# A linear-attention and feed-forward kernel: the first batch's keys loaded without a cast, its queries ahead of its values, and its first tile's pieces in another order

## The chip, the cores and the metric

The kernel runs on one core of one Trainium2 chip. The metric is the device time of one execution in microseconds (us); lower is better. The engines are named as in the profile: PE is TensorE's matmuls and PEld its weight loads, DVE is VectorE, ACT is ScalarE, POOL is GpSimd, SP is SyncE. SPq and POOLq mark the issue of a DMA by SP or POOL.

## The reference, cut to what matters

Eight batches of eight heads, 576 positions and 64 channels go through a cosine-weighted linear attention. The result, 4608 tokens by 512, goes through a feed-forward with a product of two branches.

```python
def phi(x, c, s):                      # c, s: cos and sin of pi/2 * pos / 576
    r = np.maximum(x, 0.0)
    return np.concatenate([r * c, r * s], axis=-1)
q_p, k_p = phi(q, cos_w, sin_w), phi(k, cos_w, sin_w)
kv  = np.einsum('bhsf,bhsd->bhfd', k_p, v)
num = np.einsum('bhsf,bhfd->bhsd', q_p, kv)
den = np.einsum('bhsf,bhf->bhs', q_p, k_p.sum(axis=2))[..., None] + 1e-06
x   = (num / den).transpose(0, 2, 1, 3).reshape(4608, 512)
out = (((x @ w1) * (x @ w2)) @ w3) @ w_out
```

Inputs and output are float32; the kernel computes in bf16 with float32 accumulation.

## The kernel before, in words

**Attention of a batch.** The 576 positions of a batch are five chunks, four of 128 rows and one of 64 (`c = 0..4`). A chunk's keys become features `kp`: DVE writes the cosine half with one max-and-multiply, ACT writes the sine half with a scaled Relu. Values go into `va` beside a column of ones, so that one product of `kp` with `va` gives `kv` and the denominators' sums together. The result is copied to `kvs` in bf16. A chunk's queries become features `qp` in the same way, are transposed by PE through PSUM (`pst`) into `qpT`, and multiplied with `kvs`. DVE divides by the denominators into `xblk`. PE transposes `xblk`, and a copy brings it into `xT`, the layout in which the feed-forward reads it.

**Feed-forward.** The tokens are nine tiles of 512. `ffn_groups(t)` is a generator that issues tile `t`'s matmuls: products with `w1b` and `w2b` (L512), their elementwise product `abT` (L517, L518, or L557, L561), then the product with `w34b` (L583), which is `w3 @ w_out` formed once in the kernel (L239, L251). After each group it yields, and the attention work that is planned for this slot (`at(s, ...)`) is issued behind it. So the program order of every engine is written by hand, and each engine runs its own instructions strictly in that order.

**The head of the kernel**, which the change touches, is a straight list at the end of the function, for batch 0 alone. The loads of batch 0 come in pieces. SP loads the first four heads' keys, chunks 0 to 3, as float32 without a cast (`kf` number 0, the first half), and the keys of chunk 4 (`k4`). POOL loads everything else and casts to bf16 on the way, in this order: values of the first four heads, values of chunk 4, queries of chunks 0 and 1, keys of the last four heads (`kf` number 1, the second half), values of the last four heads, queries of chunks 2 and 3, then the weights. While nothing has arrived, PE runs products of zeros (`idle_mms`, L198).

In the list, `first_keys(half)` makes four heads' key features, `first_values(half)` copies their values, `first_kv(half)` forms their `kv`; `first_num(c, half)` is four heads' numerator of a chunk, and the function that it returns normalizes it on DVE; `q_tr_halves` and `q_tr` transpose a chunk of queries (with `evac=False`, the entry `[1]` of what `q_tr` returns is the copy by ACT); `num(0, 2)` and `num(0, 3)` are whole chunks; `x_tr` brings a chunk into `xT`. `other_loads` issues the remaining weights behind the second half's `kvs`.

**Tile 0** is treated apart (`first_tile`): its 512 tokens are the chunks 0 to 3 of batch 0, and the first two column pairs are computed chunk by chunk (`chunk`), each as soon as its `xT` is there. Before the change the slots in it run so: half of chunk 0, `num(0, 2)`, the rest of chunk 0, `x_tr` of chunk 1 with `q_tr` of chunk 3, chunk 1 with its `multiply`, `x_tr` of chunk 2 and `num(0, 3)`, chunk 2, half of `on_half(0, 1)`, `x_tr` of chunk 3, the rest of it, chunk 3. `multiply` is an ACT copy out of PSUM (L517) and a DVE product (L518).

Of the kernel before, what the change touches and what calls it, by code (L numbers as in the profile page):

```python
# [16 lines left out]
P = 128  # L17
H, S, D = 8, 576, 64
F = 2 * D
# [49 lines left out]
def kernel(  # L69
# [85 lines left out]
    def load_half(eng, t, src, half, heads):  # L155

        rows = src[0, ts(half, 4), 0:512, :].rearrange("h (p j) d -> p h (j d)", j=4)
        eng.dma_start(out=t[:, heads, 0:4, :].rearrange("p h j d -> p h (j d)"), in_=rows)  # L158


    k0 = [wst.tile([P, 4, 4, D], dt, name=f"kf{i}") for i, dt in enumerate((FP32, BF16))]
    k4 = wst.tile([P, H, D], FP32, name="k4")
    q0 = raw[0, "q"] = ld.tile([P, H, NCH, D], BF16, name="qs", bufs=2)
    v0 = raw[0, "v"] = ld.tile([P, H, NCH, D], BF16, name="vs")
    load_half(nc.sync, k0[0], k, 0, slice(0, 4))
    nc.sync.dma_start(out=k4[0:64, :, :], in_=k[0, :, 512:S, :].rearrange("h p d -> p h d"))
    zeros = const.tile([P, 512], BF16, name="zeros")
    nc.vector.memset(zeros[:], 0.0)
    cosv, sinv = _trig_tables(nc, const)
    load_half(nc.gpsimd, v0, v, 0, slice(0, 4))  # L170
    va_bufs, kp_bufs, qp_bufs = [], [], []

# [22 lines left out]
    def idle_mms(n):  # L195

        for _ in range(n):
            nc.tensor.matmul(unread[:, :], lhsT=zeros[:, 0:128], rhs=zeros[:], start=True, stop=True)  # L198

    idle_mms(17)  # L200
    load_first4(nc.gpsimd, v0, v)
    load_first(nc.gpsimd, q0, q, 0, 2)
    load_half(nc.gpsimd, k0[1], k, 1, slice(0, 4))
    identb = const.tile([P, P], BF16, name="identb")
    make_identity(nc, identb[:])
    load_half(nc.gpsimd, v0, v, 1, slice(4, 8))
# [96 lines left out]
    def prep_q(b, c):  # L303
        features(b, feat_of(b)[1], raw[b, "q"], c)
        if c in dma_q(b):
            transpose_q(b, c)
# [18 lines left out]
            nc.vector.tensor_copy(out=kvs[:, 4:8, :], in_=kvt[:, 1, 0:260])  # L325
            att[b]["kvs"] = kvs

    def first_keys(half):
        kp = feat_of(0)[0]
        for c in range(4):  # L330
            src, heads = k0[half][:, :, c, :], ts(half, 4)
            nc.vector.tensor_scalar(out=kp[:, c, heads, 0:D], in0=src, scalar1=0.0,
                                    scalar2=cosv[:, c:c + 1], op0=ALU.max, op1=ALU.mult)
            nc.scalar.activation(out=kp[:, c, heads, D:F], in_=src, func=ACTF.Relu,
                                 scale=sinv[:, c:c + 1], bias=0.0)
        if half == 0:
            nc.vector.tensor_scalar(out=kp[0:64, 4, :, 0:D], in0=k4[0:64], scalar1=0.0,
                                    scalar2=cosv[0:64, 4:5], op0=ALU.max, op1=ALU.mult)
            nc.scalar.activation(out=kp[0:64, 4, :, D:F], in_=k4[0:64], func=ACTF.Relu,
                                 scale=sinv[0:64, 4:5], bias=0.0)  # L340

    def first_values(half):
        heads = ts(half, 4)
# [162 lines left out]
    def ffn_groups(t):  # L506
        x = xT[t]
        abT = fsb.tile([P, 8, 512], BF16, name="abT", bufs=2)

        def products(out, w, jc, tok):  # L510
            for kc in range(4):
                nc.tensor.matmul(out, lhsT=w[:, kc, ts(jc, 128)], rhs=x[:, kc, tok],  # L512
                                 start=(kc == 0), stop=(kc == 3))

        def multiply(a, b, pair, half):
            asb = fsb.tile([P, 512], BF16, name="asb")
            nc.scalar.copy(out=asb[:], in_=a[:, :])  # L517
            nc.vector.tensor_mul(out=abT[:, ts(pair, 2), ts(half, 256)],  # L518
                                 in0=asb[:].rearrange("p (i n) -> p i n", i=2),
                                 in1=b[:, :].rearrange("p (i n) -> p i n", i=2))  # L520

        def chunk(a, b, c):

            for i in range(2):
                for ps, w in ((a, w1b), (b, w2b)):
                    products(ps[:, ds(256 * i + 128 * (c % 2), 128)], w, i, ts(c, 128))
                if c == 0 and i == 0:
                    yield

        def on_half(half, pair):  # L530
            a, b = ffn_tile(), ffn_tile()
            for ps, w in ((a, w1b), (b, w2b)):
                for i in range(2):
                    products(ps[:, ts(i, 256)], w, 2 * pair + i, ts(half, 256))
                if w is w1b and not (t == 0 and half == 1):
                    yield
            multiply(a, b, pair, half)
            yield

        def first_tile():  # L540

            banks = [(ffn_tile(), ffn_tile()) for _ in range(2)]
            for c in range(4):
                if c == 3:
                    yield from on_half(0, 1)
                yield from chunk(*banks[c // 2], c)
                if c % 2:
                    multiply(*banks[c // 2], 0, c // 2)
                yield
            yield from whole(4)  # L550
            yield from on_half(1, 1)

        def whole(jc):
            aT = ffn_tile()
            products(aT[:, :], w1b, jc, slice(0, 512))
            asb = fsb.tile([P, 512], BF16, name="asb")
            nc.scalar.copy(out=asb[:], in_=aT[:, :])  # L557
            yield
            bT = ffn_tile()
            products(bT[:, :], w2b, jc, slice(0, 512))  # L560
            nc.vector.tensor_mul(out=abT[:, jc, :], in0=asb[:], in1=bT[:, :])  # L561
            yield

        if t == 0:
            yield from first_tile()
        elif t == 1:
            for half in range(2):
                for pair in range(2):
                    yield from on_half(half, pair)
        for jc in range((5, 4)[t] if t < 2 else 0, 8):  # L570
            yield from whole(jc)
        if t == 0:
            for jp in range(8):
                for part in range(2):
                    w34_mm(jp, part)
                    yield
            early.close()
            holds.append(ctx.enter_context(tc.tile_pool(name="hold", bufs=HELD,
                                                        reuse_waits="tile")))
        for ms in range(3 if t == NT - 1 else 4):  # L580
# [12 lines left out]
            yield  # L593
        if t == NT - 1:
            for half in range(2):
                cols = ts(half, 256)
                ops = ffn_tile()
                for jc in range(8):
                    nc.tensor.matmul(ops[:, 0:256], lhsT=abT[:, jc, ts(3, 128)],  # L599
                                     rhs=w34b[:, jc, cols], start=(jc == 0), stop=(jc == 7))  # L600
                nc.scalar.copy(out=osb[:, 1, cols], in_=ops[:, 0:256])
                store(nc.sync, osb[:, 1:2, :], 4 * t + 3, 1, cols)
                yield
# [6 lines left out]
    def at(s, *calls):  # L610
        slots[s] += calls
# [26 lines left out]
            at(s, issue)  # L638


    first_keys(0)
    first_values(0)
    first_kv(0)
    q0f = feat[0][1]
    prep_q(0, 0)
    prep_q(0, 1)
    idle_mms(2)
    q_tr_halves(0, 0)
    first_keys(1)
    halves = [first_num(0, 0)]  # L650
    q_tr(0, 1, evac=False)[1]()
    first_values(1)
    halves[0]()
    features(0, q0f, q0, 2, sin=False)
    first_kv(1)
    halves.append(first_num(1, 0))
    halves.append(first_num(0, 1))
    halves[1]()
    halves[2]()
    features(0, q0f, q0, 2, cos=False)  # L660
    q_tr(0, 2, evac=False)[1]()
    other_loads(att[0]["kvs"][:, 4, 0:1])
    halves.append(first_num(1, 1))
    x_tr(0, 0, by_vector=True)
    halves[3]()
    first.close()
    ps_ffn.append(ctx.enter_context(tc.tile_pool(name="ps_ffn1", bufs=2, space=bass.MemoryType.PSUM)))
    features(0, q0f, q0, 3)


    at(0, lambda: num(0, 2))
    at(1, lambda: x_tr(0, 1), lambda: q_tr(0, 3, evac=False)[1]())
    at(2, lambda: x_tr(0, 2, by_vector=True), lambda: num(0, 3))
    at(4, lambda: x_tr(0, 3))
    at(6, lambda: nc.vector.memset(qp_bufs[0][64:128, 4, :, :], 0.0))
    at(19, lambda: features(0, q0f, q0, 4))
# [73 lines left out]
```

## Time and profile before

| | us |
|---|---|
| median of 14 runs | 250.88 (250.54 to 252.68) |
| the profiled execution | 250.72 |
| its span in the profile | 249.0 |
| PE busy, with 1843 matmuls | 238.8 (96%) |
| DVE / ACT / POOL busy | 137.2 / 132.7 / 95.6 |
| first matmul of tile 0 | 16.37 |
| start of tile 0's fifth column block, `whole(4)` | 25.51 |
| last matmul's end | 245.84 |

The profiled execution took 250.72 us, 1.7 us more than its span; that part lies before and after what the profile records. Times within the span count from its start. A row of a timeline has start, duration, engine, line, operation, output and inputs, how many instructions were merged, and in brackets how long the engine had been idle and what released it. TensorE's granted clock is full speed in all forty slices of the span.

### The profile page before, as it was taken

To read this page: it belongs to the slowest core of one execution; us is meant where nothing else is said; L and a number is where in the kernel's file an instruction comes from. 1 tells how busy PE (TensorE), PEld (TensorE's weight loads), DVE (VectorE), ACT (ScalarE), POOL (GpSimd) and SP (SyncE) were. 2 spreads that over 40 slices of the span, in tenths; PEclk is the share of its full clock that TensorE was granted. 3 is DMA by queue.
4 is the path that set the end of the run, shared out by engine and by line. 5 is a ranking of instruction groups with operands and counts; after the bars stand their busy time and mean duration, and the time that the engine had idled before them with its cause. 6 is when DMAs were issued, how large, how long until landed. Compare 5 with 4: busy or idle time off the path is not lost.

```text
span 249.0 us, 5001 instructions
## 1 busy us (share of the span) xinstructions
PE 238.8 (96%) x1843; PEld 129.4 (52%) x1843; DVE 137.2 (55%) x347; ACT 132.7 (53%) x273; POOL 95.6 (38%) x198
## 2 busy tenths in 40 slices
PE   8578999999999999999999999999999999999994
PEld 3367545566875445454554554455545554444443
DVE  6684473486978634737575566447466635312420
ACT  7663323784954684367546644855575433434332
POOL 8773352034521341225142612173204005978700
PEclk9999999999999999999999999999999999999999
DMA  6999999999999979699999799989995436898923
GB/s 131 180 196 200 207 204 204 194 141 155 197 143 151 154 125 180 87 131 156 113 182 165 109 184 149 156 135 155 152 145 95 95 65 209 248 294 286 290 88 130
DMA packets 86232, 40.96 MB, mean 165 GB/s; under 512 B 53824, under 2 KB 82752, under 8 KB 86208
## 3 DMA queue, kind: packets, MB, share of 16 engines
q0 software_dynamic: 37552, 27.47, 71.6%
q1 hardware_dynamic: 48656, 13.18, 34.8%
q8 instruction: 14, 0.23, 0.4%
q14 instruction: 10, 0.08, 0.1%
HBM read 38.80 MB, written 9.44 MB: 194 GB/s over the span
## 4 chain that ended last, share of the span: by engine, by line
PE 91%; DMA 3%; POOL 2%; DVE 1%; ACT 1%; issue 0%; POOLq 0%
PE ffnps L512 50%; PE ffnps L583 24%; PE ffnps L251 6%; PE pnum L415 4%; PE pnum L319 4%; DMA qs<-in_q_dram 3%; PE pst L239 1%; PE ffnps L599 1%; PE pst L467 1%; POOL vs L158 1%; PE pst L389 1%; ACT asb L517 0%; ACT qpT L392 0%; POOL qs L133 0%; DVE xblk L379 0%
## 5 line engine op out<-in xcount | busy, mean ns | idle before, releaser
L512 PE MATMUL ffnps<-xT,w1b 128*128 128x512 bf16 (+2 forms) x336 | 75.0, 348 | 2.1 <-DVE xT L469 1.5
L512 PE MATMUL ffnps<-xT,w2b 128*128 128x512 bf16 (+2 forms) x336 | 75.0, 348 | 0.0
L561 DVE TENSOR_TENSOR abT<-asb,ffnps 128x512 bf16<-128x512 bf16 x64 | 43.9, 686 | 52.8 <-PE ffnps L512 52.3
L583 PE MATMUL ffnps<-w34b,abT 128*128 128x512 bf16 x280 | 65.0, 379 | 0.0
L557 ACT CAST asb<-ffnps 128x512 bf16<-128x512 f32 x64 | 37.4, 584 | 50.7 <-PE ffnps L512 45.8
L512 PEld LDWEIGHTS <-w1b 128*128 128x128 bf16 x336 | 30.6, 98 | 28.6 <-issue 2.6
L512 PEld LDWEIGHTS <-w2b 128*128 128x128 bf16 x336 | 30.7, 98 | 27.4
L618 POOL COPY seen<-mark 1x1 bf16<-1x1 bf16 x50 | 8.9, 177 | 82.9 <-ACT mark L616 82.8
L583 PEld LDWEIGHTS <-abT 128*128 128x128 bf16 x280 | 26.0, 98 | 27.9 <-DVE abT L561 0.2
L590 ACT COPY osb<-ffnps 128x512 f32<-128x512 f32 x35 | 20.5, 584 | 35.8 <-PE ffnps L583 35.8
L288 ACT ACTIVATE qp<-qs,sinv 128x512 bf16<-128x512 bf16 (+1 forms) x40 | 28.3, 720 | 0.0
L311 POOL COPY va<-vs 128x512 bf16<-128x512 bf16 (+1 forms) x30 | 17.8, 626 | 26.0 <-DMA vs<-in_v_dram 17.9
L433 DVE TENSOR_TENSOR xblk<-pnum,den 128x512 bf16<-128x512 f32 (+1 forms) x36 | 24.9, 691 | 1.2
L288 ACT ACTIVATE kp<-ks,sinv 128x512 bf16<-128x512 bf16 (+1 forms) x35 | 25.0, 717 | 0.3 <-DMA ks<-in_k_dram 0.3
L497 POOL DMA_DIRECT2D out_dram<-osb x42 | 22.1, 531 | 2.2 <-issue 2.1
L415 PEld LDWEIGHTS <-qpT 128*128 128x128 bf16 x304 | 14.8, 98 | 8.1
L431 DVE TENSOR_SCALAR den<-pnum 128x8 f32<-128x8 f32 (+1 forms) x36 | 5.9, 163 | 22.3 <-PE pnum L415 22.0
L284 DVE TENSOR_SCALAR qp<-qs,cosv 128x512 bf16<-128x512 bf16 (+1 forms) x40 | 17.0, 435 | 0.7 <-DMA qs<-in_q_dram 0.6
L251 PE MATMUL ffnps<-woutb,w3T 128*128 128x512 bf16 x64 | 15.9, 380 | 0.0
L415 PE MATMUL pnum<-kvs,qpT 128*128 128x65 bf16 x288 | 15.4, 194 | 0.0
L319 PEld LDWEIGHTS <-kp 128*128 128x128 bf16 x280 | 11.4, 98 | 4.1
L284 DVE TENSOR_SCALAR kp<-ks,cosv 128x512 bf16<-128x512 bf16 (+1 forms) x35 | 12.8, 374 | 0.0
(96 smaller groups left out, 183.9 us busy)
## 6 DMA issues: line engine op xcount, KB each, us to landing
out_dram<-osb POOLq DMA_DIRECT2D x16, 256.0 KB, 4.2
out_dram<-osb POOLq DMA_DIRECT2D x24, 128.0 KB, 3.7
vs<-in_v_dram POOLq DMA_DIRECT2D x8, 256.0 KB, 5.9
qs<-in_q_dram POOLq DMA_DIRECT2D x8, 256.0 KB, 6.3
ks<-in_k_dram POOLq DMA_DIRECT2D x6, 320.0 KB, 5.5
qs<-in_q_dram POOLq DMA_DIRECT2D x6, 320.0 KB, 5.9
vs<-in_v_dram POOLq DMA_DIRECT2D x6, 320.0 KB, 5.9
ks<-in_k_dram POOLq DMA_DIRECT2D x6, 256.0 KB, 6.4
```

The lines of the kernel that those rows point to most:

```text
L251: nc.tensor.matmul(acc[:, :], lhsT=w3T[:, lc, :], rhs=woutb[:, lc, :], start=(lc == 0), stop=(lc == 7))
L284: nc.vector.tensor_scalar(out=dst[:R, c, :, 0:D], in0=src[:R, :, c, :], scalar1=0.0, scalar2=cosv[:R, at:at + 1], op0=ALU.max, op1=ALU.mult)
L288: nc.scalar.activation(out=dst[:R, c, 0:n, D:F], in_=src[:R, 0:n, c, :], func=ACTF.Relu, scale=sinv[:R, at:at + 1], bias=0.0)
L319: nc.tensor.matmul(kvt[:, h // 4, ds((h % 4) * 65, 65)], lhsT=kp[:, c, h, :], rhs=va[:, c, h, 0:D + 1], start=(i == 0 and h % 4 == 0), sto ...
L415: nc.tensor.matmul(banks[h // 4][:, ds((h % 4) * 65, 65)], lhsT=qpT[:, h, ds(at, 128)], rhs=kvs[:, h, :], start=True, stop=True)
L433: nc.vector.tensor_tensor(out=xblk[rows, g], in0=n4[:, :, :, 0:D], in1=den[rows, g].unsqueeze(3).to_broadcast([R, G, 4, D]), op=ALU.mult)
L497: eng.dma_start(out=rows[:, :, cols], in_=osb[64 * i:64 * i + rows.shape[0], :, cols])
L512: nc.tensor.matmul(out, lhsT=w[:, kc, ts(jc, 128)], rhs=x[:, kc, tok], start=(kc == 0), stop=(kc == 3))
L557: nc.scalar.copy(out=asb[:], in_=aT[:, :])
L561: nc.vector.tensor_mul(out=abT[:, jc, :], in0=asb[:], in1=bT[:, :])
L583: nc.tensor.matmul(ops[:, :], lhsT=abT[:, jc, ts(ms, 128)], rhs=w34b[:, jc, :], start=(jc == 0), stop=(jc == 7))
L590: nc.scalar.copy(out=osb[:, ms % 2, :], in_=ops[:, :])
```

## The change

Four things are altered, all in the head and in tile 0.

- **Loads.** Both halves of batch 0's keys are loaded in float32 by SP, the second between the first and `k4`. On POOL's queue the second half of the keys is gone, and the queries of chunks 0 and 1 come first, ahead of the values.
- **The list.** All key features come first, those of the second half included. The second half's sine features are shared out: chunks 0, 1 and 2 by ACT, chunk 3 by DVE. The features of query chunks 0 and 1 come between them, then the transposes, and only then values and `kv`. The features of query chunk 2 go ahead of the first normalization on DVE, those of chunk 3 ahead of the last one.
- **Idle products.** Twenty-five at the start instead of seventeen, and the two in the list are gone.
- **Tile 0.** `num(0, 2)` runs ahead of the first chunk. Chunk 1 is given a yield in its middle and chunk 2 loses the one at its end, so `x_tr` of chunk 2 comes in the middle of chunk 1, ahead of chunk 1's `multiply`, and `num(0, 3)` behind chunk 1.

```diff
-    k0 = [wst.tile([P, 4, 4, D], dt, name=f"kf{i}") for i, dt in enumerate((FP32, BF16))]
+    k0 = [wst.tile([P, 4, 4, D], FP32, name=f"kf{i}") for i in range(2)]
...
-    load_half(nc.sync, k0[0], k, 0, slice(0, 4))
+    for half in range(2):
+        load_half(nc.sync, k0[half], k, half, slice(0, 4))
     nc.sync.dma_start(out=k4[0:64, :, :], in_=k[0, :, 512:S, :].rearrange("h p d -> p h d"))
...
+    load_first(nc.gpsimd, q0, q, 0, 2)
     load_half(nc.gpsimd, v0, v, 0, slice(0, 4))
...
-    idle_mms(17)
+    idle_mms(25)
     load_first4(nc.gpsimd, v0, v)
-    load_first(nc.gpsimd, q0, q, 0, 2)
-    load_half(nc.gpsimd, k0[1], k, 1, slice(0, 4))
...
-    def first_keys(half):
+    def first_keys(half, cos=(), sin=(), sin_by_vector=()):
...
+        for c in sin_by_vector:
+            R, heads, src = of(c)
+            nc.vector.tensor_scalar(out=kp[R, c, heads, D:F], in0=src, scalar1=0.0,
+                                    scalar2=sinv[R, c:c + 1], op0=ALU.max, op1=ALU.mult)
...
-                if c == 0 and i == 0:
+                if c < 2 and i == 0:
                     yield
...
-                yield
+                if c != 2:
+                    yield
...
-    first_keys(0)
+    q0f = feat_of(0)[1]
+    first_keys(0, cos=range(4), sin=range(4))
+    first_keys(1, cos=range(5), sin=(4, 0))
+    features(0, q0f, q0, 0)
+    first_keys(1, sin_by_vector=(3,))
+    features(0, q0f, q0, 1)
+    first_keys(1, sin=(1, 2))
+    q_tr_halves(0, 0)
+    by_scalar = q_tr(0, 1, evac=False)[1]
     first_values(0)
     first_kv(0)
-    q0f = feat[0][1]
-    prep_q(0, 0)
-    prep_q(0, 1)
-    idle_mms(2)
-    q_tr_halves(0, 0)
-    first_keys(1)
+    by_scalar()
     halves = [first_num(0, 0)]
-    q_tr(0, 1, evac=False)[1]()
     first_values(1)
+    features(0, q0f, q0, 2, sin=False)
     halves[0]()
-    features(0, q0f, q0, 2, sin=False)
     first_kv(1)
     halves.append(first_num(1, 0))
+    halves[1]()
     halves.append(first_num(0, 1))
-    halves[1]()
     halves[2]()
     features(0, q0f, q0, 2, cos=False)
-    q_tr(0, 2, evac=False)[1]()
+    by_scalar = q_tr(0, 2, evac=False)[1]
     other_loads(att[0]["kvs"][:, 4, 0:1])
     halves.append(first_num(1, 1))
     x_tr(0, 0, by_vector=True)
+    by_scalar()
+    features(0, q0f, q0, 3)
     halves[3]()
     first.close()
...
-    features(0, q0f, q0, 3)
-
-
-    at(0, lambda: num(0, 2))
+    num(0, 2)
+
+
     at(1, lambda: x_tr(0, 1), lambda: q_tr(0, 3, evac=False)[1]())
-    at(2, lambda: x_tr(0, 2, by_vector=True), lambda: num(0, 3))
+    at(2, lambda: x_tr(0, 2, by_vector=True))
+    at(3, lambda: num(0, 3))
     at(4, lambda: x_tr(0, 3))
```

More of the change, by code (lines that the diff above doesn't have):

```diff
@@ L326, in kv_chunk, with of @@
             att[b]["kvs"] = kvs
-    def first_keys(half):
+    def first_keys(half, cos=(), sin=(), sin_by_vector=()):
         kp = feat_of(0)[0]
[L330 to L340, printed above, removed]
+        def of(c):
+            if c < 4:
+                return slice(0, P), ts(half, 4), k0[half][:, :, c, :]
+            return slice(0, 64), slice(0, H), k4[0:64]
+        for c in cos:
+            R, heads, src = of(c)
+            nc.vector.tensor_scalar(out=kp[R, c, heads, 0:D], in0=src, scalar1=0.0,
+                                    scalar2=cosv[R, c:c + 1], op0=ALU.max, op1=ALU.mult)
+        for c in sin:
+            R, heads, src = of(c)
+            nc.scalar.activation(out=kp[R, c, heads, D:F], in_=src, func=ACTF.Relu,
+                                 scale=sinv[R, c:c + 1], bias=0.0)
+        for c in sin_by_vector:
+            R, heads, src = of(c)
+            nc.vector.tensor_scalar(out=kp[R, c, heads, D:F], in0=src, scalar1=0.0,
+                                    scalar2=sinv[R, c:c + 1], op0=ALU.max, op1=ALU.mult)
     def first_values(half):
```

## The prediction

> **What bounds the kernel now.** First the stretches: the busy time of each engine up to tile 0's first matmul, from there to the start of `whole(4)`, and from there to PE's end.
>
> ```profile
> 0.00:16.37 16.37, 10.95 (x103) 6.02 (x104) 11.66 (x51) 11.92 (x22) 12.45 (x26) 1.00 1.20 165
> 16.37:25.51 9.14, 7.52 (x116) 6.93 (x116) 4.91 (x14) 4.13 (x7) 4.88 (x8) 1.00 1.40 199
> 25.51:245.84 220.33, 220.29 (x1624) 116.47 (x1623) 120.68 (x284) 116.31 (x245) 78.30 (x166) 1.00 1.06 164
> ```
>
> The first figure after the stretch is its length, the second PE's busy time. From 25.51 us on PE is idle for 0.04 us in 220. The change leaves those matmuls alone. So the time follows the start of `whole(4)` one to one, as long as no later load comes too late; everything is decided in the first 25 us. There I read the chain that ended last, then the timeline.
>
> ```profile
> 6.16 7.50 DMA qs<-in_q_dram
> 16.37 0.61 PE ffnps L512 x8
> 20.07 0.69 DVE abT L518
> 24.87 0.59 ACT asb L517
> ```
>
> ```profile
> 7.36 0.72 ACT L339 ACTIVATE kp<-k,sinv 64x512 bf16<-64x512 f32 x1 [0.99 <-DMA k<-in_k_dram]
> 9.55 0.94 DVE L284 TENSOR_SCALAR qp<-qs,cosv 128x512 bf16<-128x512 bf16 x2 [0.63 <-DMA qs<-in_q_dram]
> 10.38 0.61 PE L402 MATMUL pst<-identb,qp 128*128 128x128 bf16 x8 [0.68 <-ACT qp L288]
> 13.68 0.35 DVE L284 TENSOR_SCALAR qp<-qs,cosv 128x512 bf16<-128x512 bf16 x1
> 15.12 1.01 ACT L392 COPY qpT<-pst 128x1024 bf16<-128x1024 bf16 x1 [0.71 <-PE pst L389]
> 20.67 0.42 DVE L469 COPY xT<-pst 128x512 bf16<-128x512 bf16 x1
> 21.14 0.38 PE L512 MATMUL ffnps<-xT,w1b 128*128 128x128 bf16 x4 [1.02 <-DVE xT L469]
> ```
>
> The chain runs through the load of query chunks 2 and 3, landing at 13.66, and then through short steps to 16.37. In tile 0 PE loses 1.02 us, because the copy of chunk 2 into `xT` (20.67) stands on DVE behind chunk 1's `multiply` (20.07).
>
> The DMA view, by issue and by queue, gives the landings. First the two loads by SP with size and time to landing; then packets, MB and share of each queue in the stretches 3.75 to 4.25, 7.75 to 8.25 and 5.75 to 6.75.
>
> ```profile
> kf<-in_k_dram SPq DMA_DIRECT2D x1, 512.0 KB, 3.8
> k<-in_k_dram SPq DMA_DIRECT2D x1, 128.0 KB, 6.1
> ```
>
> ```profile
> q1 hardware_dynamic: 209, 0.07, 55.6%
> ```
>
> ```profile
> q0 software_dynamic: 362, 0.09, 185.7%
> ```
>
> ```profile
> q0 software_dynamic: 340, 0.12, 103.7%
> q1 hardware_dynamic: 91, 0.02, 17.5%
> ```
>
> SP's queue (q1) moves 209 packets in 0.5 us while it is alone, and 91 in 1.0 us beside POOL's casting queue (q0). Issue plus time to landing: `kf` first half 4.5 us, `k4` 7.35, values first half 7.7, queries 0 and 1 9.56, keys second half 10.8, values second half 12.2, queries 2 and 3 13.66.
>
> **What the Trainium skill says.** "DMA: Bandwidth & Descriptors", section "SWDGE vs HWDGE vs iDMA": a cast during a DMA is to be had from GpSimd alone, and each DMA engine takes turns between the hardware and the software queue; q1's fall beside q0 agrees with that. "SBUF — State Buffer", section "Who interferes with whom": VectorE's two-port modes and GpSimd shut each other out; agrees with L284, which takes 0.35 us at 13.68 and 0.71 at 16.98, where POOL issues a DMA. "TensorE: Matmul & The Clock Gate", section "What's actually happening": an idle window of some 3.4 us halves the clock; here no gap is longer than 1.4 us, and the clock is full.
>
> **The change, part by part.**
>
> *Loads.* POOL issues one transfer fewer in the head (0.80 us of issuing at 3.94), and queries 0 and 1 go out at 1.47. SP's three transfers have 3 x 512 packets and 48 completions, 1584. Before, q1 had moved 744 by 4.25 us, when q0 began; at the same pace 840 are left. Alone they need 840/418 = 2.0 us, `k4` landing at 6.7 (0.4 us from last packet to landing, as before). At 91 a us they need 9.2 us, landing at 13.9. In strict turns with q0's 256 B packets a pair costs 1/418 + 1/724 us, which is 265 a us: 3.2 us, landing at 7.8. I take **7.9**; 7.4 to 9.2 for the range. POOL's stream: queries 0 and 1 then share with the same packets and land at 8.2; behind them follow values (1.33 us, as from `kf` to values before), chunk 4 (0.4), values (1.34) and queries 2 and 3 (1.45), which land at **12.7**, 1.0 earlier than before. The casting queue has one load less, but takes turns for longer: 12.3 to 13.7.
>
> *The list*, walked by the durations of before, each engine in its order. At `k4`'s landing K, ACT still owes chunk 4's sine (0.63 to the next start), one second-half sine (0.41) and query chunk 0's sine (0.77 with the handing on): transposes at K + 1.8. DVE's second-half cosines (4 x 0.31 in float32, 0.20 in bf16 before) end before K; its chunk 4 cosine (0.71), two query cosines and the sine of chunk 3 (0.31) end within the same 1.8 or just behind it. Then PSUM to `qpT` 0.44, buffer free for chunk 1's transposes 0.46, these 0.45, sixteen `kv` products 0.64, chunk 4's and their drain 0.33: `kvs` copy at K + 4.15. The copy 0.42, numerator 0.17, the second half's twenty products and drain 0.97: second `kvs` copy at K + 5.7. Copy 0.29, query chunk 2's sine 0.76, transposes 0.65, `qpT` copy 1.07: `num(0, 2)` at K + 8.5. It takes 0.36, chunk 0 takes 0.86: `x_tr` of chunk 1 at K + 9.7, which is 17.6 (17.52 before). First tile-0 matmul at 16.74 against 16.37, but with `num(0, 2)` already done. The four value copies and chunk 4's (0.7 us on DVE) lie under this; the eight added idle products end at 8.6, before the transposes at 9.7, and cost nothing; if the transposes came first, each would cost 0.22.
>
> *Tile 0.* `x_tr` of chunk 1, copy by ACT: 1.06, chunk 1 at 18.66. Its halves are 0.43 each; `x_tr` of chunk 2 (0.23) between them lets DVE copy at 19.5, ahead of `multiply` at 20.4. `num(0, 3)` (0.36) and chunk 2 follow with no gap: the 1.02 us are gone. Late next is `x_tr` of chunk 3: its normalization now stands behind `multiply` (20.36 + 0.60 + 1.16 = 22.1), so PE waits 0.3 after half of `on_half` (ends 21.8). Then 0.23 + 0.86 + chunk 3 (0.43, 0.42 to the ACT copy) + 0.62: `whole(4)` at K + 16.8, that is **24.7** against 25.51.
>
> The second chain is the landing Q of queries 2 and 3: DVE now makes their cosine (0.27) ahead of three normalizations (0.74 each); `xT` copy, `qc3` and the fourth follow, and `whole(4)` comes at Q + 11.9, 24.6 for Q = 12.7. The two are level, so missing either by half a us shows in full. The same walk in the old order, with the old landings, ends at 25.5, as measured. I set 24.8, **0.7 earlier**. The profiled 250.72 becomes 250.0; the median of the runs lies 0.16 above that execution, so 250.2.
>
> *Later loads* have room: the first `w3` block lands at 25.9 and is used at 32.4, and POOL's stream comes earlier too. POOL's marker for `other_loads` waits for the second `kvs`, at 14.0 instead of 13.8, while the loads issued before it keep the DMA engines fed until about 19. Nothing is charged.
>
> **The rivals.** (a) *The keys' queue starves*: `k4` waits behind a whole second half and beside the cast queue, and the features of query chunk 0 wait behind `k4` on both engines. It decides from K = 25.5 - 16.8 = 8.7; at K = 9.2 the time is 0.5 longer (251.4), at 11 us it is 2.3 longer (253.2). For it: q1's 91 a us, and that nothing of ACT's or DVE's can pass. Against: before, most of `k4` went through by 5 us, and q0's first load now has small packets. (b) *No net change*: queries 2 and 3 land at 13.3 to 13.7, since the DMA engines move the same bytes; the reordering saves 1.0 in tile 0 and loses as much ahead of it: 250.6 to 250.9. For it: Q rules alone at 11.9 behind its landing. (c) *K early*, under 7.4: DVE's cosines and the queries then rule, and the floor is Q + 11.9 with Q = 12.3: 249.6.
>
> **How the numbers follow.** About 0.2%, 0.5 us, is what a measurement of this kernel can tell from none. Forecast and (c) together 0.54 for faster by more; (b), with the forecast's own misses of 0.3 us in a walk of some forty steps, 0.27; (a) 0.19. The predicted time is the forecast's, 250.2, its own range 249.7 to 250.7. The range goes from (c) less 0.2, 249.4, to (a) at 9.2 us and a little over, 251.5; outside lies (a) in its full form and a floor broken, together under 2 in 10.
>
> **What would show it.** `k4` landing at 7.5 to 8.3 and queries 2 and 3 at 12.3 to 13.1; the first transposes near 9.7; no wait of PE for the copy of chunk 2, a new one of about 0.3 us ahead of `x_tr` of chunk 3; `whole(4)` at 24.8; PE dense behind it. Wrong if ACT and DVE stand idle for `k4` beyond 8.7, if PE's gap in tile 0 stays, or if a gap opens after 25 us.

## The result, and the profile after

After the change the kernel takes **253.59 us** (median of 10 runs, 252.72 to 256.48), beside 250.91 before (47 runs). The ratio is 1.0112, with a 95% interval of 1.0094 to 1.0131. I had put 250.2, so the sign is wrong as well, and the time lies outside the range. Runs that lie over 1.5% above the fastest of their kernel count in the medians given here but not in the ratios: three of 20 with `k4` by POOL, one of four with tile 0's old order. The profiled execution took 253.22 us, with a span of 251.4.

First the stretches again: up to tile 0's first matmul, to the start of `whole(4)`, and to PE's end. The columns are length, busy time of PE, PEld, DVE, ACT and POOL with instructions, PE's clock, DMA share and GB/s.

```profile
0.00:19.51 19.51, 13.51 (x118) 7.97 (x119) 13.19 (x53) 11.61 (x21) 11.91 (x25) 0.91 1.23 184
19.51:27.56 8.05, 7.19 (x113) 6.51 (x110) 4.37 (x13) 4.04 (x7) 5.63 (x9) 1.00 1.31 193
27.56:247.88 220.32, 220.28 (x1624) 116.44 (x1623) 121.49 (x284) 116.26 (x245) 76.75 (x164) 1.00 1.06 162
```

The last stretch is as long as before, 220.32 against 220.33, and as dense. The middle one lost 1.09 us (9.14 to 8.05): 0.83 is the old gap of 1.02 less a new one of 0.19, and the rest is `num(0, 2)`, which now runs ahead of it, in the first stretch. The first one grew by 3.14 us (16.37 to 19.51), and its clock fell from 1.00 to 0.91. `whole(4)` starts 2.05 later; the rest of the span's 2.4 is the tail behind PE's last matmul, 3.5 against 3.2.

The chain that ended last (start, length, step) has changed its origin: it began with the load of query chunks 2 and 3, and now begins with `k4`.

```profile
1.79 8.28 DMA k<-in_k_dram
10.09 1.12 ACT kp L343 x2
13.94 1.11 PE pnum L366 x20
18.17 1.02 ACT qpT L400
```

In the timeline of the same kernel the bracket at the end of a row gives how long the engine had stood idle and what released it.

```profile
10.09 0.72 ACT L343 ACTIVATE kp<-k,sinv 64x512 bf16<-64x512 f32 x1 [3.67 <-DMA k<-in_k_dram]
10.09 0.48 DVE L339 TENSOR_SCALAR kp<-k,cosv 64x512 bf16<-64x512 f32 x1 [2.24 <-DMA k<-in_k_dram]
11.12 1.32 ACT L288 ACTIVATE qp<-qs,sinv 128x512 bf16<-128x512 bf16 x2
11.88 0.96 PE L410 MATMUL pst<-identb,qp 128*128 128x128 bf16 x8 [3.17 <-ACT qp L288]
13.73 1.31 PE L366 MATMUL pnum<-va,kp 128*128 128x65 bf16 x20
14.58 0.35 DVE L284 TENSOR_SCALAR qp<-qs,cosv 128x512 bf16<-128x512 bf16 x1
15.07 0.38 ACT L369 CAST kvs<-pnum 128x260 bf16<-128x260 f32 x1 [1.84 <-PE pnum L366]
22.32 0.42 DVE L477 COPY xT<-pst 128x512 bf16<-128x512 bf16 x1 [1.09 <-PE pst L475]
23.16 0.69 DVE L526 TENSOR_TENSOR abT<-asb,ffnps 128x512 bf16<-128x512 bf16 x1 [0.42 <-ACT asb L525]
24.95 0.40 PE L475 MATMUL pst<-identb,xblk 128*128 128x128 bf16 x4 [0.19 <-DVE xblk L441]
```

ACT stood still for 3.67 us and DVE for 2.24 until `k4` landed at 10.09. Behind that, in both engines' order, are the features of query chunk 0, so PE's transposes start at 11.88, after 3.17 us with one matmul in them. At 14.58 DVE takes up queries 2 and 3, just behind their landing and with no wait shown, so the keys' chain is the longer one. Queries 0 and 1 are late as well: by the issues below they landed at 10.07, with `k4` (9.56 before). Of the 1.50 us by which the transposes start later than before (11.88 against 10.38) they account for 0.5. The other 1.0 us is what ACT spends on key features between `k4`'s landing and chunk 0's sine, at 11.12. In tile 0 the copy of chunk 2 into `xT` (22.32) now stands ahead of `multiply` (23.16), and PE waits only 0.19 us, ahead of `x_tr` of chunk 3.

The DMA issues of the same kernel, with size and time to landing, in the order second half of the keys, `k4`, queries 0 and 1, queries 2 and 3:

```profile
kf<-in_k_dram SPq DMA_DIRECT2D x1, 512.0 KB, 4.9
k<-in_k_dram SPq DMA_DIRECT2D x1, 128.0 KB, 8.3
qs<-in_q_dram POOLq DMA_DIRECT2D x1, 256.0 KB, 8.6
qs<-in_q_dram POOLq DMA_DIRECT2D x1, 256.0 KB, 9.2
```

With the issue times 1.25, 1.79, 1.47 and 5.33 this gives landings at 6.15, 10.09, 10.07 and 14.53. The last three had been forecast at 7.9, 8.2 and 12.7. Before, `k4` landed at 7.35 and queries 2 and 3 at 13.66.

Last, what each queue moved (packets, MB, share), q1 being SP's and q0 POOL's, in the stretches 0 to 5, 5 to 5.75, 5.75 to 6.25, 6.25 to 8.25 and 8.25 to 9.75 us.

```profile
q1 hardware_dynamic: 974, 0.98, 58.4%
...
q1 hardware_dynamic: 80, 0.07, 33.6%
q0 software_dynamic: 52, 0.01, 24.2%
...
q0 software_dynamic: 160, 0.04, 98.7%
q1 hardware_dynamic: 7, 0.00, 2.6%
...
q0 software_dynamic: 796, 0.22, 105.0%
q1 hardware_dynamic: 430, 0.11, 39.6%
...
q0 software_dynamic: 736, 0.26, 146.6%
q1 hardware_dynamic: 92, 0.02, 11.4%
```

By 6.25 us q1 has moved 1061 packets, about the two halves' 1056 (2 x 512 and 32 completions). The rest is `k4`: 430 packets in 2.0 us, then 92 in 1.5 us.

### The profile page after: what moved, and what is told of

Read it like the earlier page. It is cut to its first block, busy times and chain, and to the rows that moved or that the text cites. A ratio compares the mean times of both kernels' runs of the same rounds, so it can differ in the third digit from the quotient of the medians.

```text
span 251.4 us, 5010 instructions
## 1 busy us (share of the span) xinstructions
PE 241.0 (96%) x1849; PEld 130.9 (52%) x1849; DVE 139.1 (55%) x348; ACT 132.3 (53%) x272; POOL 94.3 (38%) x197
## 4 chain that ended last, share of the span: by engine, by line
PE 91%; DMA 3%; ACT 3%; DVE 1%; SPq 0%; issue 0%
PE ffnps L520 49%; PE ffnps L592 24%; PE ffnps L251 6%; PE pnum L423 4%; PE pnum L319 4%; DMA k<-in_k_dram 3%; PE pst L239 1%; PE pst L397 1%; PE pnum L366 1%; PE ffnps L608 1%; PE pst L475 1%; ACT qp L288 0%; ACT asb L525 0%; ACT kp L343 0%; ACT qpT L400 0%; SPq L158 0%
## 5 line engine op out<-in xcount | busy, mean ns | idle before, releaser
L520 PE MATMUL ffnps<-xT,w1b 128*128 128x512 bf16 (+2 forms) x336 | 75.0, 348 | 0.7 <-ACT asb L525 0.5
L520 PE MATMUL ffnps<-xT,w2b 128*128 128x512 bf16 (+2 forms) x336 | 75.0, 348 | 0.0
L520 PEld LDWEIGHTS <-w2b 128*128 128x128 bf16 x336 | 30.7, 98 | 27.4
L520 PEld LDWEIGHTS <-w1b 128*128 128x128 bf16 x336 | 30.5, 98 | 27.0 <-issue 0.9
L311 POOL COPY va<-vs 128x512 bf16<-128x512 bf16 (+1 forms) x30 | 17.6, 622 | 24.0 <-PE ffnps L520 12.7
L284 DVE TENSOR_SCALAR qp<-qs,cosv 128x512 bf16<-128x512 bf16 (+1 forms) x40 | 18.0, 458 | 0.0
L423 PE MATMUL pnum<-kvs,qpT 128*128 128x65 bf16 x288 | 15.4, 194 | 0.6 <-ACT qpT L400 0.6
```

What stands on the lines that cost most here:

```text
L284: nc.vector.tensor_scalar(out=dst[:R, c, :, 0:D], in0=src[:R, :, c, :], scalar1=0.0, scalar2=cosv[:R, at:at + 1], op0=ALU.max, op1=ALU.mult)
L423: nc.tensor.matmul(banks[h // 4][:, ds((h % 4) * 65, 65)], lhsT=qpT[:, h, ds(at, 128)], rhs=kvs[:, h, :], start=True, stop=True)
```

## The experiments

Theory one: `k4`, third on SP's queue, is held up by turns with POOL's casting queue, and everything in the list waits for it. Theory two: PE's idle time ahead of the transposes costs clock on top. Theory three: tile 0's new order brings its 1.0 us. The rivals are named with each experiment. Line numbers L469, L512, L518 in kernels built from before are L477, L520, L526 in those built from after. All ratios are to the kernel before, on the same chip.

### Tile 0's order alone

The edit is the last part of the change put into the kernel before.

```diff
-                if c == 0 and i == 0:
+                if c < 2 and i == 0:
                     yield
...
-                yield
+                if c != 2:
+                    yield
...
-    at(0, lambda: num(0, 2))
+    num(0, 2)
...
-    at(2, lambda: x_tr(0, 2, by_vector=True), lambda: num(0, 3))
+    at(2, lambda: x_tr(0, 2, by_vector=True))
+    at(3, lambda: num(0, 3))
```

> The kernel before with only the new order in tile 0: num(0, 2) ahead of the first chunk, a yield in the middle of chunk 1, none at the end of chunk 2, num(0, 3) one slot later. Loads, list and idle products as before. Theory (this part was priced right and its gain was only covered up): PE's gap of 1.02 us ahead of chunk 2 goes, whole(4) starts at 24.5 instead of 25.5, and the time is 1.0 us under the kernel before, about 249.9. Rival (the gap only moves, since x_tr of chunk 3 then waits for a normalization behind the multiply): whole(4) within 0.3 us of 25.5, time within 0.3 us of the kernel before.

Measured: 250.27 us (18 runs), ratio **0.9959, 0.9942 to 0.9977**. The timeline of this kernel:

```profile
19.67 0.42 DVE L469 COPY xT<-pst 128x512 bf16<-128x512 bf16 x1 [0.56 <-PE pst L467]
20.51 0.69 DVE L518 TENSOR_TENSOR abT<-asb,ffnps 128x512 bf16<-128x512 bf16 x1 [0.41 <-ACT asb L517]
22.29 0.40 PE L467 MATMUL pst<-identb,xblk 128*128 128x128 bf16 x4 [0.16 <-DVE xblk L433]
24.91 1.02 PE L512 MATMUL ffnps<-xT,w1b 128*128 128x512 bf16 x3 [0.45 <-ACT asb L517]
```

The copy is ahead of `multiply`, the 1.02 us gap is gone, 0.16 us comes in its place, and `whole(4)` is at 24.91 instead of 25.51, though in this run `k4` and the queries landed 0.3 to 0.4 us later than in the profile of before. Theory three holds. This part alone is faster than both kernels.

### The loads alone, and the queries ahead of the values alone

The first edit puts the change's loads into the kernel before, with the old list; the second only moves the queries to the head of POOL's queue and leaves both key loads as they were.

```diff
# loads alone
-    load_half(nc.sync, k0[0], k, 0, slice(0, 4))
+    for half in range(2):
+        load_half(nc.sync, k0[half], k, half, slice(0, 4))
...
# both kernels
+    load_first(nc.gpsimd, q0, q, 0, 2)
     load_half(nc.gpsimd, v0, v, 0, slice(0, 4))
...
     load_first4(nc.gpsimd, v0, v)
-    load_first(nc.gpsimd, q0, q, 0, 2)
...
# loads alone
-    load_half(nc.gpsimd, k0[1], k, 1, slice(0, 4))
```

> The kernel before with only the new loads: both key halves in float32 by SP ahead of the keys of chunk 4, queries 0 and 1 first on POOL's queue. List, idle products and tile 0 as before. Theory (the loads are what costs): keys of chunk 4 land near 10.1 us as in the changed kernel, the old list needs them first of all, so whole(4) comes 3.2 us later than in the kernel before, about 28.7, or 29.4 if PE's clock also falls in its longer idle time: 254 to 255 us, worse than the whole change. Rival (the new list is what costs): the loads alone give within 0.5 us of the kernel before.

> The kernel before with one edit of the loads: queries 0 and 1 at the head of POOL's queue, ahead of the values; the second half of the keys stays on POOL's queue. Theory (the order on POOL's queue alone is nearly free; it is the second half of the keys on SP's queue that costs): queries 0 and 1 land near 8.3, values near 9.3, queries 2 and 3 at 13.7 as before; whole(4) within 0.5 us of 25.5 and the time within 0.5 us of the kernel before. Rival (small 256 B packets at the head of POOL's queue, or the late values, are what costs): over 1 us slower than the kernel before.

Measured: the loads alone 256.31 us (4 runs), 1.0194 (1.0142 to 1.0245); the queries first 254.42 (4 runs), 1.0112 (1.0072 to 1.0153). Timeline rows and one stretch of the first, then a row of the second:

```profile
9.50 0.72 ACT L339 ACTIVATE kp<-k,sinv 64x512 bf16<-64x512 f32 x1 [3.10 <-DMA k<-in_k_dram]
10.58 0.69 PE L358 MATMUL pnum<-va,kp 128*128 128x65 bf16 x16 [3.56 <-DVE va L345]
```

```profile
12.00:16.00 4.00, 2.90 (x30) 2.31 (x30) 2.50 (x11) 3.73 (x8) 0.00 (x0) 0.51 1.52 193
```

```profile
10.31 0.63 DVE L345 COPY va<-vs 128x256 bf16<-128x256 bf16 x4 [3.74 <-DMA vs<-in_v_dram]
```

The loads alone cost more than I expected (254 to 255). The old list wants values first; with the queries ahead they land at 10.3 instead of 7.7, and PE stands idle for 3.56 us and then runs at half clock. The queries' place costs about 3 us by itself in the old list; I had expected it nearly free, and the rival with the late values held. So the loss doesn't come from the other parts of the change taken together: with the same loads the new list, the idle products and tile 0's order are about 2.1 us better than the old ones (the ratios 1.0112 and 1.0194 are apart by more than their intervals). About 1.0 us of that is tile 0's order, by the experiment above; the list by itself was not run.

### Which key transfer is third

The kernel after, with `k4` second on SP's queue and the second half third.

```diff
-    for half in range(2):
-        load_half(nc.sync, k0[half], k, half, slice(0, 4))
+    load_half(nc.sync, k0[0], k, 0, slice(0, 4))
     nc.sync.dma_start(out=k4[0:64, :, :], in_=k[0, :, 512:S, :].rearrange("h p d -> p h d"))
+    load_half(nc.sync, k0[1], k, 1, slice(0, 4))
```

> The changed kernel with one transfer moved: on SP's queue the keys of chunk 4 stand ahead of the second half of the keys, as close to the front as before the change. Theory one (ACT and DVE wait in order for the keys of chunk 4, which were late because 512 packets of the second half stood ahead of them): they land by 8 us, the first transposes come near 10 us with the landing of queries 0 and 1, PE's clock stays full, and the time falls by 1.2 to 2 us, to 251.5 to 252.4. Theory two (the whole stream of loads is late, whichever transfer is first): queries 2 and 3 still land near 14.5 us and bound whole(4) at 26.4: a fall of 1.2 us at most, and none below 252.3. Rival (the second half, now last, takes the place of chunk 4 as the late one): less than 0.5 us gained.

Measured: 254.51 us (4 runs), 1.0147 (1.0096 to 1.0199), no gain. Timeline:

```profile
10.50 0.51 ACT L343 ACTIVATE kp<-kf,sinv 128x256 bf16<-128x256 f32 x1 [3.50 <-DMA kf<-in_k_dram]
10.50 1.27 DVE L339 TENSOR_SCALAR kp<-kf,cosv 128x256 bf16<-128x256 f32 x4 [4.14 <-DMA kf<-in_k_dram]
```

The wait has moved from `k4` to the second half, which now lands at 10.50 instead of 6.15. The rival held: what stands third is late, whichever it is, and the list needs all three.

### SP's queue by itself

A copy of one column on POOL reads the second half before POOL issues its first load, so q0 begins only behind that half.

```diff
+    landed = sm.tile([P, 1], FP32, name="landed", bufs=1)
+    nc.gpsimd.tensor_copy(out=landed[:], in_=k0[1][:, 0, 0, 0:1])
     load_first(nc.gpsimd, q0, q, 0, 2)
```

> The changed kernel with a wait ahead of POOL's first load: a one-column copy that reads the second half of the keys, so that POOL issues nothing before these have landed. A measurement, not a candidate. Theory (turns with POOL's queue delay the keys of chunk 4): with SP's queue alone its three transfers land at 4.6, 6.1 and 7.2 or earlier, against 10.1 in the changed kernel; queries 0 and 1 are issued near 6.2 and land at 10.5 or later, and the time is 1 us or more above the changed kernel. Rival (512 packets of 256 B are slow by themselves): chunk 4's keys land past 9 us with nothing beside them.

Measured: one run, 255.33 us, which says little more than that late queries and values cost more than an early `k4` saves (the transposes start at 12.54). What it was run for is the landing. A row of its timeline, then q1 in the stretches 4.75 to 5.75 and 5.75 to 8.25:

```profile
7.05 0.72 ACT L345 ACTIVATE kp<-k,sinv 64x512 bf16<-64x512 f32 x1 [0.64 <-DMA k<-in_k_dram]
```

```profile
q1 hardware_dynamic: 586, 0.24, 92.5%
...
q1 hardware_dynamic: 86, 0.02, 3.9%
```

Left alone, the same three transfers bring `k4` at **7.05**. What q0 has under way beside them costs the other 3.0 us (2.3 to 3.5 by the landings in the five kernels with the change's loads).

### The chunk-4 keys off SP's queue

In the kernel after, `k4` becomes bf16 and is loaded, with a cast, by POOL at the head of its queue; a second kernel gives this one 29 idle products instead of 25.

```diff
-    k4 = wst.tile([P, H, D], FP32, name="k4")
+    k4 = wst.tile([P, H, D], BF16, name="k4")
...
-    nc.sync.dma_start(out=k4[0:64, :, :], in_=k[0, :, 512:S, :].rearrange("h p d -> p h d"))
...
+    nc.gpsimd.dma_start(out=k4[0:64, :, :], in_=k[0, :, 512:S, :].rearrange("h p d -> p h d"))
     load_first(nc.gpsimd, q0, q, 0, 2)
...
# second kernel
-    idle_mms(25)
+    idle_mms(29)
```

> The changed kernel with the keys of chunk 4 taken from SP's queue and put at the head of POOL's, cast to bf16. SP then carries the two key halves alone. Theory (what was late is whatever stands third on SP's queue, because its packets take turns with POOL's first load on the DMA engines): chunk 4's keys land by 7.5 us, queries 0 and 1 near 9, the first transposes at 9.6 to 9.9, with the clock full; whole(4) is then set by the landing of queries 2 and 3 near 13.7, at 25.6, and the time is 1.5 to 2.3 us under the changed kernel, near that of the kernel before. Rival (all transfers of the head are late together, whatever the queue): queries 0 and 1 still land at 10, queries 2 and 3 at 14.5, whole(4) at 26.4 or later: 1.2 us less than the changed kernel at most, mostly by the clock.

> The kernel with the keys of chunk 4 at the head of POOL's queue (otherwise the changed kernel), and 29 idle products instead of 25, ending near 9.3 us instead of 8.4. Theory (its runs spread from 249.8 to 255 because a late landing lets PE idle for over 3 us and the clock falls): the slow runs become rarer, the median comes to 249.9 to 250.5, about 0.4% under the kernel before, and PE's start is delayed by 0.1 us at most, which the landing of queries 2 and 3 covers. Rival (the spread is that of the landings themselves): median and spread stay as they were, within 0.2% of the kernel before.

Measured: 251.24 us (20 runs, 249.78 to 254.98), 0.9993 (0.9967 to 1.0020), and with 29 products 250.96 (22 runs, 249.83 to 252.91), 0.9985 (0.9965 to 1.0005). Timeline of the first:

```profile
6.89 0.72 ACT L343 ACTIVATE kp<-k,sinv 64x512 bf16<-64x512 bf16 x1 [0.49 <-DMA k<-in_k_dram]
8.49 1.33 ACT L288 ACTIVATE qp<-qs,sinv 128x512 bf16<-128x512 bf16 x2 [0.48 <-DMA qs<-in_q_dram]
9.27 0.62 PE L410 MATMUL pst<-identb,qp 128*128 128x128 bf16 x8 [0.87 <-ACT qp L288]
13.14 0.35 DVE L284 TENSOR_SCALAR qp<-qs,cosv 128x512 bf16<-128x512 bf16 x1 [0.80 <-DMA qs<-in_q_dram]
24.65 1.02 PE L520 MATMUL ffnps<-xT,w1b 128*128 128x512 bf16 x4 [0.45 <-ACT asb L525]
```

One transfer moved from one queue to the other undoes the loss: 1.0112 becomes 0.9993. It isn't `k4` alone that comes earlier: queries 0 and 1 are there at 8.5, against 10.07 in the kernel after, though they are second on their queue now. In the profiled execution (249.9 us) the times are near those that I had forecast for the change itself: transposes at 9.3, queries 2 and 3 at 13.1, `whole(4)` at 24.65, which is Q + 11.5. But its runs scatter, and the granted clock of each shows why in part. Of the 17 runs up to 253.5 us, the seven with a mean clock of 0.998 or more have a median of 250.04, the ten with less 251.7. Four more idle products bring 18 of 22 runs to 0.998 or more and take the upper tail away; the median is hardly lower, against what I had expected. Landings that differ from run to run may be what remains (in the two profiled executions `k4` came at 6.89 and 7.28, queries 2 and 3 at 13.14 and 13.73); the runs without a trace don't show it.

### The list's order for the chunk-4 features

The kernel after, loads untouched, with chunk 4's key features behind those of query chunks 0 and 1.

```diff
-    first_keys(1, cos=range(5), sin=(4, 0))
+    first_keys(1, cos=range(4), sin=(0,))
     features(0, q0f, q0, 0)
     first_keys(1, sin_by_vector=(3,))
     features(0, q0f, q0, 1)
-    first_keys(1, sin=(1, 2))
+    first_keys(1, cos=(4,), sin=(4, 1, 2))
```

> The changed kernel with the features of chunk 4's keys moved on both engines behind those of query chunks 0 and 1; all loads as in the changed kernel. Theory one (the place of the wait costs: what stands behind chunk 4's keys in order could have run): query features start with their own landing near 10 us, first transposes near 10.9 instead of 11.9, the clock falls later or not at all, and the time is 1 to 1.5 us under the changed kernel; queries 2 and 3, landing near 14.5, then hold whole(4) at 26.4. Theory two (queries 0 and 1 land just as late as chunk 4's keys, so the order is not what costs): under 0.5 us gained beyond the clock.

Measured: 251.93 us (13 runs), 1.0036 (1.0007 to 1.0065). Timeline:

```profile
9.30 1.33 ACT L288 ACTIVATE qp<-qs,sinv 128x512 bf16<-128x512 bf16 x2 [2.49 <-DMA qs<-in_q_dram]
25.41 1.02 PE L520 MATMUL ffnps<-xT,w1b 128*128 128x512 bf16 x3 [0.45 <-ACT asb L525]
```

ACT now goes on with the queries as they land, the transposes start at 10.08 and the clock of this execution is 0.999. `k4` landed at 9.4 in it, so in the old order, at K + 1.8, they would have begun at 11.2. Two thirds of the loss is gone with no byte moved otherwise, part of it by the clock, since PE now stands idle for less. The late `k4` hurts because the transposes stand behind it in the order of ACT and DVE.

### More idle products

The kernel after with 38 idle products instead of 25, so that PE is busy until the transposes.

```diff
-    idle_mms(25)
+    idle_mms(38)
```

> The changed kernel with 38 idle products instead of 25, ending near 11.5 us, just ahead of the first transposes at 11.9. Theory (PE's clock fell to half in the 3.2 us of idle time and made the first 3.6 us of work slower): the granted clock is full from 11.9 us on, whole(4) starts 0.7 us earlier, near 26.9, and the time is about 252.9. Rival (the slow clock lay beside waits for ACT and DVE and cost nothing): full clock, and the same 253.6.

Measured: 252.35 us (9 runs), 1.0049 (1.0016 to 1.0082). Here are two stretches of the kernel after, PE's gap and what follows it, and then a stretch and three timeline rows of this one.

```profile
8.70:11.87 3.17, 0.01 (x1) 0.00 (x0) 1.40 (x4) 1.78 (x4) 1.36 (x2) 1.00 1.64 186
11.87:15.50 3.63, 3.07 (x36) 2.81 (x37) 2.48 (x12) 1.79 (x5) 0.47 (x1) 0.53 1.55 192
```

```profile
12.00:16.00 4.00, 3.24 (x66) 2.72 (x64) 3.06 (x15) 1.97 (x5) 0.00 (x0) 1.00 1.53 193
```

```profile
12.12 0.61 PE L410 MATMUL pst<-identb,qp 128*128 128x128 bf16 x8
14.41 0.38 ACT L369 CAST kvs<-pnum 128x260 bf16<-128x260 f32 x1 [1.94 <-PE pnum L366]
26.90 1.02 PE L520 MATMUL ffnps<-xT,w1b 128*128 128x512 bf16 x3 [0.45 <-ACT asb L525]
```

In the kernel after, PE's clock is 0.53 for 3.6 us behind the gap; here it stays at 1.00. From the first transposes to `whole(4)` it takes 15.68 us there (11.88 to 27.56) and 14.78 here. All of the 0.9 us lies ahead of the first copy of `kvs` (L369): 3.19 us from the transposes to it there, 2.29 here. But these transposes begin late: the products themselves hold them up (`k4` landed at 9.33, so they could have begun at 11.1), and ACT and DVE get ahead meanwhile. In three kernels at full clock without this delay the same piece takes 2.46 to 2.53 us (both with `k4` by POOL, and the one with chunk 4's features behind). So theory two holds, at **0.7 to 0.9 us**. Counted from `k4`'s landing, this execution gains nothing (17.57 us to `whole(4)`, 17.47 in the kernel after), since the late transposes take back what the clock gives. The gain stands in the runs: each of the kernel after's has a mean clock of 0.993 or less, each of these 0.997 or more, and the ratio drops from 1.0112 to 1.0049, which is 1.6 us. That is more than one such stretch of half clock costs; five of the ten runs of the kernel after have a mean clock of 0.985 or less, about twice the loss of the profiled one (0.992). This execution, at 253.15 us one of the longer of the nine, lost another 0.6 us behind `whole(4)`, with no releaser named for most of it; for the time itself the nine runs are the better witness.

### Two that tell less

The kernel before with tile 0's new order, both key halves by SP and `k4` at the head of POOL's queue, but queries behind the values and the old list. Of its edit, the new first load of POOL:

```diff
+    nc.gpsimd.dma_start(out=k4[0:64, :, :], in_=k[0, :, 512:S, :].rearrange("h p d -> p h d"))
     load_half(nc.gpsimd, v0, v, 0, slice(0, 4))
```

> The kernel before with the new order in tile 0, both key halves in float32 by SP, and the keys of chunk 4 at the head of POOL's queue, cast; values and queries behind them in the old order, the old list. A candidate for a version ahead of both. Theory (with two transfers SP's queue is done by 6.2 us, POOL's stream carries 384 KB less, so queries 2 and 3 land near 13.0): whole(4) at 24.0 to 24.4, the time 1.2 to 1.6 us under the kernel before. Rival (turns at the start make chunk 4's keys and the first values late, 7.8 and 9 us, and the old list needs both first): whole(4) at 25 or later, no better than the tile 0 order alone.

Measured: 251.55 us (22 runs), 1.0012 (0.9989 to 1.0035). `k4` landed at 7.88 and values at 9.25 in the profiled execution. That execution was the longest of the 22. PE stood idle for 3.05 us ahead of its first products of keys and values, ran at half clock from 10.98 to 21.22 us, and `whole(4)` came at 28.39. The stretch from 12 to 16:

```profile
12.00:16.00 4.00, 3.56 (x44) 3.10 (x44) 3.37 (x14) 3.14 (x7) 0.00 (x0) 0.50 1.48 195
```

The second half without a cast, with `k4` by POOL, brings the old list nothing; it takes back the 0.4% that tile 0's order gives alone.

And the kernel after with tile 0's old order, which is the first experiment's diff undone:

> The changed kernel with the old order in tile 0 (num(0, 2) inside the first chunk, the old yields, num(0, 3) behind x_tr of chunk 2); loads, list and idle products as changed. Theory (the tile 0 order is worth its 1.0 us here too): PE's gap ahead of chunk 2 is back with 1.0 us, whole(4) at 28.4 to 28.6 instead of 27.6, the time 1.0 us over the changed kernel. Rival (with everything 2 us late, DVE has caught up and the order no longer matters): within 0.4 us of the changed kernel.

Measured: 254.87 us (4 runs, 252.54 to 257.12), 1.0109 (1.0055 to 1.0162). The gap of 1.02 us ahead of chunk 2 is back in the trace (24.14 to 25.16), and from the first transposes to `whole(4)` it takes 17.2 us instead of 15.7, of which the gap is 1.0. The four times scatter by more than that and can't price it: the ratio is the same as the whole change's.

## Why the prediction was wrong

**The step that failed is "*Loads*", where it says "In strict turns with q0's 256 B packets a pair costs 1/418 + 1/724 us, which is 265 a us: 3.2 us, landing at 7.8. I take 7.9".** `k4` landed at 10.09. The working had three branches, and the measured value fell between the two slower ones. The lower one was nearly right for what it described: alone, 6.7 forecast and 7.05 measured. Strict turns were the wrong model: q1 got 430 packets in 2.0 us (215 a us) while q0 got 398 a us, and then 61 a us against 491. That last rate is not only a matter of turns. A transfer ends with 16 completions, which I read as one from each of the 16 DMA engines, and it has landed with the last of them. In the trace the eighth of `k4`'s came at 8.71, the twelfth at 8.86, and the last four at 9.18, 9.32, 9.84 and 10.07: in the last 1.5 us ever fewer engines had packets of it left. My working took one rate for all, as if the 16 ended together. The kernel before already had such a spread: the eighth of `k4`'s completions at 5.45 there, the last at 7.33. Ahead of that lay a stretch that no branch had, 5.0 to 6.25 us, in which the two queues together moved 299 packets in 1.25 us, fewer than q1 moves alone. Of the 2.3 us by which `k4` missed my turns, about 0.9 was lost there (87 packets of q1 where 265 a us gives 331), 0.4 at 215 a us (430 packets in 2.0 instead of 1.6), and 1.15 on the last 92; q1's better start, 974 packets by 5 us where my working has 943, gave 0.1 back. The range for K ended at 9.2, under the one figure that the profile showed for q1 beside q0, 91 a us, which gave 13.9. I set that aside because q0's first packets would be small.

The same step had queries 0 and 1 at 8.2 and 2 and 3 at 12.7; they landed at 10.07 and 14.53. I had counted a load less on POOL's queue as a gain of 1.0 us. "Takes turns for longer" stood in the text as the opposite term, but the 0.9 us by which 2 and 3 were later than before don't show it: 13 of their 16 completions had come by 13.41 (13.56 before), and only the last three, up to 14.55 (13.66 before), were late.

**The second missing term is the clock.** "Here no gap is longer than 1.4 us, and the clock is full" was true of the profiled execution of the kernel before (of 43 later runs of it, 16 have a mean clock of 0.993 or less) and was carried over, because the transposes were expected at 9.7. With K at 10.09 PE was idle for 3.17 us, and the walk lost 0.7 to 0.9 us more. "TensorE: Matmul & The Clock Gate", section "What's actually happening", speaks of an idle window of some 3.4 us that free-runs; gaps of 2.78 to 3.29 us were enough in five executions here, so the shorter measured figures are the ones to plan with. Had rival (a) carried this term, it would have had its number: K = 10.1 less 8.7 is 1.4 us, with 0.7 to 0.9 for the clock 2.1 to 2.3, where `whole(4)` moved by 2.05.

**What was right.** The transposes at K + 1.8: 11.88 from 10.09, to the hundredth. `whole(4)` at K + 16.8: 26.9, and 27.56 less the clock's 0.7 to 0.9 is 26.7 to 26.9. Tile 0: its gap of 1.02 us gone, a new one of 0.19 for 0.3 forecast, about 1.0 us saved, alone a ratio of 0.9959. One to one from `whole(4)` on: 220.32 us against 220.33. The later loads: no gap of PE behind 27.56. The eight added idle products cost nothing, as said; more of them would even have helped.

**The rivals.** (a), the keys' queue starves, is what happened, by the mechanism that was named: ACT and DVE stood idle for `k4` beyond 8.7, and nothing of theirs could pass. But it had the queries 0 and 1 on time, and they landed together with `k4`. It got 0.19, the least of the three shares, although the profile showed q1 at 91 packets a us beside q0. (b), no net change, had queries 2 and 3 at 13.3 to 13.7 as its cause; they were later still, but the chain of the keys was longer. (c), `k4` early, was met only when the cast queue held off, at 7.05, or when POOL carried `k4`, at 6.89. In this second case `whole(4)` came at 24.65, where the forecast had 24.7, but by luck: there Q + 11.5 rules, with Q = 13.14, and the forecast had K + 16.8 with K = 7.9. My Q + 11.9 was 0.4 too long; it was 11.5 in three kernels that Q ruled.

**What stays open.** Why the DMA engines moved so little between 5.0 and 6.25 us is seen and not explained. It goes with three transfers on SP's queue beside POOL's: in the six kernels that have them so, q0 moved 0.03 to 0.06 MB from 5.0 to 6.0 us, in the six with two 0.09 to 0.14. "DMA: Bandwidth & Descriptors", section "SWDGE vs HWDGE vs iDMA", says that the engines take turns between the queues; the counts here agree that q1 falls when q0 runs, and not with equal turns. Landings under the same loads also differ between executions: in the five kernels with the change's loads `k4` came at 9.33 to 10.56 and queries 2 and 3 at 13.5 to 15.4. For the queries most of it lies in the last three of the 16 completions (the thirteenth came at 13.3 to 13.6 in all five). Why some lag was not found.

## What to carry to other kernels

A transfer's landing on one queue depends on what another queue has under way at that time, and it is that of the last of its completions, not of the middle one: let the range reach as far as the lowest rate that the profile shows for that pair of queues (13.9 us here, against 10.1 measured), and put what is needed first where it shares with the least. In engines that run in order, work for a late operand goes behind the work that doesn't need it; that alone, with the clock that it kept, gave back two thirds here. If a forecast lets PE stand idle for some 3 us, the half clock behind the gap belongs into the sum.

## What the runs showed of the hardware

- By 5.75 us SP's queue, left alone, had moved 1498 of its 1584 packets (all but the last 86); beside POOL's casting queue 1054. The rest took it another 4 us there, 215 packets a us from 6.25 us on and 61 a us at the end, when the last engines finished.
- The loss of clock comes in whole pieces. Seven profiled executions show half clock, for 3.4 us (the kernel after and two more), 6.8 (one) or 10.2 (three). PE's gap ahead of it was 2.78 to 4.00 us, and half clock began between 0.9 us before the gap's end and 1.5 us behind it; in the six executions at full clock the longest gap was 1.77 us. A mean clock of 0.993, the commonest value under full, fits one such piece: 0.007 x 251 us at half speed is some 3.5 us. 0.985 and 0.978 fit two and three.
- In the kernel with the queries first, 15 of the 16 completions of the first values had come by 8.66 us and the last came at 10.28, and the landing is that of the last. The five other loads of POOL that landed by 14.9 us end with the same lag of 1.6 us. Other executions have other lags or none: the queries 2 and 3 of the kernel before end with 13.59, 13.62 and 13.66.
